# Fused sparse attention and softplus MLP: where in a step the put-off work is taken up

## The chip, the cores and the metric

The kernel runs on one NeuronCore of one Trainium2 chip. The metric is device time in microseconds for one execution of the whole program. The core has five engines that run their own instruction queues side by side: TensorE (matrix products and transposes, PE in the profile; its weight loads are PEld), VectorE (DVE), ScalarE (ACT), GpSimd (POOL) and SyncE (SP, which here issues the DMAs). An instruction waits at the head of its engine's queue until what it reads has been written and what it overwrites has been read.

## The reference

Attention for 8 batches of 8 heads, 576 rows of 64 each, in which each row keeps only the scores that lie within tau of its maximum; the result goes, as 4608 tokens of 512, through two matrices with a softplus between.

```python
scores = scale * np.matmul(q, k.transpose(0, 1, 3, 2))
thresh = np.max(scores, axis=-1, keepdims=True) - tau
scores = np.where(scores >= thresh, scores, -1000000000.0)
attn = np.exp(scores - np.max(scores, axis=-1, keepdims=True))
attn = attn / (np.sum(attn, axis=-1, keepdims=True) + 1e-09)
x = np.matmul(attn, v)          # then (4608, 512)
h = x @ w_in                    # (512, 2048)
g = np.maximum(h, 0.0) + np.log1p(np.exp(-np.abs(h)))
return g @ w_out                # (2048, 512)
```

All of it is float32. The kernel gets that precision from float32r products by splitting an operand into a rounded high part and the rest, a low part, and adding two or three products.

## The kernel before

**Tiles.** A *unit* is one batch and one pair of heads: 32 units. Each has 9 tiles of 128 query rows by 576 keys (4 of each head and one, number 4 of the unit, that holds the last 64 rows of both). The 288 tiles are walked in one loop (L963), one *step* a tile. The feed-forward part is a Python generator (`stream`, L794): it yields after every matmul, so that a step takes a quota of feed-forward matmuls (L967, L985). The quotas follow the table `Q9` over the nine steps of a unit, and 512 tokens make a chunk, which starts a few steps after its attention is done.

**A step.** What a step emits, and in which order, is a string of letters. Steps 0 to 35 use `PAT0`; steps 36 to 287 use `PAT`, which is `ThRlefmpfxSvwp`:

- `T` `weights_T` (L477): TensorE transposes the masked exponentials of this tile (L493; in every second tile of a pair also L490, for the 64 columns left over of both). They land in the PSUM bank that held the tile's scores.
- `h` `weights_hi` (L512): ScalarE casts the transposed weights to their high part gH; in every second tile of a pair it makes one more copy for the left-over columns.
- `R` `row_max` (L446): VectorE takes the maximum of the next tile's scores (negm) and the threshold (thr).
- `l` `weights_lo` (L536): VectorE makes the low part gL of this tile; in second tiles also two short subtractions (out gH).
- `e` `exps` (L453): ScalarE, the exponentials of the next tile. `m` `mask` (L457): VectorE, masks them and sums the row (e_all).
- `f`: half of the quota of feed-forward matmuls (L664, L666, L668 for the first product, L732 for the second).
- `x` `extras` (L908): once in a while the value products of a finished group (`values`, L561, lines L574 to L576), transposes of the next unit's k and q (L375, L377, L383), the reciprocal of the row sums, loads.
- `S` `scores` (L425): TensorE, the scores of the tile after the next (L442), into the bank that this step's h and l have read.
- `v`, `w`: products and weight preparation that occur only early in the kernel.
- `p` `point` (L834): takes up the put-off work that is due.

**Put-off work.** `defer(n, f)` (L828) puts f off by n points. What reads a result of TensorE is put off by one point, so that it isn't queued before the result is near: the casts of the transposed k and q (`qkT`, `queries`, `qkT_rest`: ScalarE, and for q two DMAs by SyncE), the softplus of two finished banks (`softplus`, L679: ScalarE), one point later the split of its result into g high (VectorE) and g low (GpSimd) (`parts_of`, L703), the sums of the second product into acc (`project_out`, L740: VectorE), the output of a value group (`values_out`, L579: ScalarE copies one half of a PSUM bank to xp, VectorE adds the other half), the row sums' way through DRAM (`row_scales_out`, L598: ScalarE, SyncE), and later the scaling and storing of xp (GpSimd, SyncE). None of it issues an instruction of TensorE. The string has two points a step: one behind `m`, one at the end.

**What sets the order.** The framework plans the order of each engine's instructions by emission order and by its own reckoning of when an instruction can start. From step 72 (`TQ`) on, `Queue` (L149) ties each VectorE and each ScalarE instruction behind the one emitted before it, so these two engines keep the order of the string; TensorE's order stays the planner's, which may put a matmul that it reckons ready ahead of one that is emitted earlier and isn't. Value groups are issued by `x` at tiles 2, 5, 7 and, for the last one, at tile 0 of the next unit; transposes of the next unit's k and q at tiles 3, 4, 6 and 8.

ScalarE's exponential and softplus need different activation tables: where one follows the other, a table load stands between.

Of the kernel before, what the change touches and what calls it, by code (L numbers as in the profile page):

```python
# [30 lines left out]
XD = 3  # L31
LS = 4
LAG0 = 5
PAT = "ThRlefmpfxSvwp"
PAT0 = "RMTeShlfpfxvwp"
WD = 4
ST = (1, 3, 4, 4, 5, 6, 6, 8)
# [23 lines left out]
def tile_kernel(ctx: ExitStack, tc: tile.TileContext, q, k, v, tau, w_in, w_out, out):  # L61
# [901 lines left out]
    for g, (cur, t) in enumerate(tiles):  # L963
# [5 lines left out]
        upto = done  # L969
        for step in PAT0 + ("m" if g == TG - 1 else "") if g < TG else PAT:  # L970
            if step == "T":
# [13 lines left out]
            elif step == "f":  # L985
                upto += quota / PAT.count("f")
                while done < upto:
# [51 lines left out]
```

## Time and profile before

| | us |
|---|---|
| median of 3 runs | 1431.99 (1431.76 to 1434.83) |
| profiled execution | 1432.59 |
| its span, first to last instruction | 1430.8 |
| TensorE busy in the span | 1386.3 |
| VectorE busy | 988.3 |
| ScalarE busy | 847.9 |
| GpSimd busy | 588.0 |

In the profile a line of the timeline gives the start in us, the time taken, the engine, the line of the kernel, the operation, what it writes and reads, shapes and the number of instructions merged; in brackets the engine's idle time before it and what ended it. Nearly all VectorE and ScalarE instructions are called through `Queue` and so bear its line, L156: they are told apart by what they write. Matmul ends are modelled, and matmuls overlap: the step from one start to the next tells more than the time taken. Lines of the waits give who waited for whom, the total in us, how often, and the longest.

### The profile page before, as it was taken

Reading aid. Unit: us, or ns where it says so; the run is one execution under the profiler, and the core shown is the slowest. Engines: PE = TensorE matmul, PEld = TensorE weight load, DVE = VectorE, ACT = ScalarE, POOL = GpSimd, SP = SyncE. Lnnn points to the kernel's source line nnn. Section 1 sums busy time; section 2 is a strip of 40 time slices with the busy share of each in tenths; the row PEclk is TensorE's granted clock in tenths of the full one; section 3 lists DMA queues with packets and bytes.
Section 4 is the critical chain, followed back from the end, with each engine's and each line's share of the span. In section 5 each row is a group of like instructions: output and inputs, shape, how many; then the busy total and the mean of one; then the engine's idle time right before and its main releaser. Section 6 shows DMA issues by size and latency. Waiting matters only on the chain.

```text
span 1430.8 us, 23585 instructions
## 1 busy us (share of the span) xinstructions
PE 1386.3 (97%) x7860; PEld 1166.4 (82%) x7860; DVE 988.3 (69%) x2211; ACT 847.9 (59%) x1615; POOL 588.0 (41%) x619
## 2 busy tenths in 40 slices
PE   6988899999999999999999999999999999999998
PEld 4655688788888888888888888888888888788886
DVE  6887688787777777787778777777777777402111
ACT  6766767667666576667665666667666765211110
POOL 3666666534333433344333433344333531323221
PEclk9999999999999999999999999999999999999999
DMA  5766766435333534445443533444434532343421
GB/s 169 222 188 210 221 198 185 126 91 180 111 103 111 155 103 125 120 128 159 117 118 91 165 107 108 127 138 122 122 112 134 157 96 84 101 137 111 135 79 44
DMA packets 131209, 189.94 MB, mean 133 GB/s; under 512 B 35312, under 2 KB 86800, under 8 KB 131088
## 3 DMA queue, kind: packets, MB, share of 16 engines
q1 hardware_dynamic: 131088, 188.43, 45.0%
q8 instruction: 63, 1.03, 0.3%
q14 instruction: 58, 0.48, 0.1%
HBM read 140.51 MB, written 27.41 MB: 117 GB/s over the span
## 4 chain that ended last, share of the span: by engine, by line
PE 82%; DVE 4%; DMA 3%; issue 3%; POOL 3%; ACT 2%; SPq 2%; POOLq 0%; ACTq 0%; DVEq 0%
PE o L732 25%; PE s L442 11%; PE h L666 9%; PE h L668 8%; PE h L664 8%; PE s L493 7%; PE pv L574 4%; PE pv L575 3%; PE tr L383 2%; PE pv L568 2%; DVE e_all L156 1%; DMA qn<-in_q_dram 1%; PE pv L576 1%; PE s L490 1%; DVE negm L156 1%
## 5 line engine op out<-in xcount | busy, mean ns | idle before, releaser
L732 PE MATMUL o<-wo_o,g 128*128 128x512 f32 x1728 | 446.0, 400 | 0.4 <-POOL g L133 0.4
L732 PEld LDWEIGHTS o<-wo_o,g 128*128 128x128 f32 x1728 | 313.5, 188 | 59.7 <-POOL g L133 1.1
L133 POOL TENSOR_TENSOR g<-st,g 128x512 fp32r<-128x512 f32 x144 | 189.7, 1337 | 242.9 <-DVE g L156 224.5
L156 ACT CAST gH<-s 128x512 fp32r<-128x512 f32 (+2 forms) x432 | 179.6, 467 | 144.2 <-PE s L493 118.2
L156 DVE SCALAR_TENSOR_TENSOR e_all<-s,thr,e_all 128x576 f32<-128x576 f32 x288 | 235.2, 817 | 40.7 <-ACT e_all L156 36.4
L666 PE MATMUL h<-xl,wi 128*128 128x512 f32 x576 | 231.9, 403 | 4.6 <-POOL xl L133 4.6
L156 ACT ACTIVATE e_all<-s,negm 128x576 f32<-128x576 f32 x288 | 216.2, 751 | 32.6 <-PE tr L490 15.5
L664 PE MATMUL h<-xh,wi 128*128 128x512 f32 x576 | 232.5, 404 | 2.1 <-ACT xh L156 1.6
L156 DVE TENSOR_REDUCE negm<-s 128x1 f32<-128x576 f32 x288 | 215.6, 748 | 26.1 <-PE s L442 22.5
L668 PE MATMUL h<-xh,wi 128*128 128x512 f32 x576 | 229.0, 398 | 0.0
L156 DVE TENSOR_TENSOR gL<-s,gH 128x512 fp32r<-128x512 f32 (+1 forms) x270 | 169.1, 635 | 47.7 <-ACT gH L156 39.5
L442 PE MATMUL s<-kT,qT 128*128 128x288 f32 x1024 | 194.3, 311 | 7.4 <-ACT gH L156 3.8
L156 DVE CAST g<-st 128x512 fp32r<-128x512 f32 x128 | 57.7, 492 | 170.6 <-ACT st L156 170.6
L442 PEld LDWEIGHTS s<-kT,qT 128*128 128x128 f32 x1024 | 149.7, 191 | 23.6 <-issue 5.3
L493 PE MATMUL s<-identr,e_all 128*128 128x128 f32 x1008 | 151.4, 272 | 0.0
L156 ACT ACT_TABLE_LOAD x111 | 142.4, 1283 | 7.5 <-PE h L668 5.5
L156 ACT ACTIVATE st<-h 128x512 f32<-128x512 f32 x144 | 78.3, 596 | 112.4 <-PE h L668 111.8
L666 PEld LDWEIGHTS h<-xl,wi 128*128 128x128 f32 x576 | 108.4, 188 | 26.8 <-POOL xl L133 6.2
L664 PEld LDWEIGHTS h<-xh,wi 128*128 128x128 f32 x576 | 108.3, 188 | 26.7 <-ACT xh L156 3.4
L493 PEld LDWEIGHTS s<-identr,e_all 128*128 128x128 f32 x1008 | 119.3, 140 | 10.6 <-DVE e_all L156 2.6
L668 PEld LDWEIGHTS h<-xh,wi 128*128 128x128 f32 x576 | 108.3, 188 | 22.3
L574 PE MATMUL pv<-gH,vt 128*128 128x256 f32 (+1 forms) x432 | 118.3, 296 | 0.2 <-ACT gH L156 0.2
(94 smaller groups left out, 1839.4 us busy)
## 6 DMA issues: line engine op xcount, KB each, us to landing
wi<-wi_d SPq DMA_DIRECT2D x144, 512.0 KB
qT<-qT SPq DMA_DIRECT2D x124, 128.0 KB
R<-r_d SPq DMA_DIRECT2D x64, 144.0 KB
kn<-in_k_dram SPq DMA_DIRECT2D x32, 256.0 KB
qn<-in_q_dram SPq DMA_DIRECT2D x32, 256.0 KB
vn<-in_v_dram SPq DMA_DIRECT2D x32, 256.0 KB
wc_i<-in_moe_w_in_dram SPq DMA_DIRECT2D x16, 512.0 KB
wi_d<-wc_i SPq DMA_DIRECT2D x32, 256.0 KB
```

The source lines that it names most:

```text
L133: eng.tensor_tensor(out=out_, in0=in_, in1=hi.bitcast(F32), op=ALU.subtract)
L156: i = getattr(self.eng, name)(*args, **kwargs)
L383: nc.tensor.transpose(pr[:, c * P:(c + 1) * P], src, identr)
L442: i = nc.tensor.matmul(sp[:, hf, 0:HS], lhs, s.kT[j][:, k0 + hf * HS:k0 + (hf + 1) * HS], start=(m == 0), stop=(m == len(parts) - 1))
L493: nc.tensor.matmul(main[:, c, :], e[:, c0:c0 + P], ident, is_transpose=True, start=True, stop=True)
L568: slow.append([lambda c=c: nc.tensor.matmul(o[0:D, 0:n], s.vn[:, 5 * j + c, :], h[:, c, 0:n].bitcast(F32), start=(c == 0), stop=(c == NC)) ...
L574: nc.tensor.matmul(o[:, 0:n], vt[:, c, :], h[:, c, 0:n], start=(c == 0), stop=False)
L575: nc.tensor.matmul(o[:, 0:n], vt[:, c, :], l[:, c, 0:n], start=False, stop=False)
L664: nc.tensor.matmul(h, wi[:, 0, cc, :], u.h[cc], start=(cc == 0), stop=False)
L666: nc.tensor.matmul(h, wi[:, 0, cc, :], u.l[cc], start=False, stop=False)
L668: nc.tensor.matmul(h, wi[:, 1, cc, :], u.h[cc], start=False, stop=(cc == NCC - 1))
L732: nc.tensor.matmul(o, u.g[fc][m // 2][:, sl], wo[fc][:, m % 2, :], start=(n == 0), stop=(n == 3 * QF - 1))
```

## The change

The second point of a step of `PAT` is emitted behind `R` of the next step instead of at the end. The first, behind `m`, stays. A step still has two points, and the work that falls due at each is the same.

```diff
-PAT = "ThRlefmpfxSvwp"
+PAT = "ThRplefmpfxSvw"
 PAT0 = "RMTeShlfpfxvwp"
```

So the order of emission over the border of two steps is, before and after:

```
before  ... m p f x S v w p | T h R l e f m p ...
after   ... m p f x S v w   | T h R p l e f m p ...
```

Nothing else changes. At step 36, the first that uses `PAT`, the point that ends step 35 (`PAT0`) is followed by one behind `R`; the last step has no point behind its products, and what is left is taken up by the points after the loop (L1004).

## The prediction

> **What bounds the kernel now.** I read the page first (the shares of the engines, TensorE far ahead), then the busy time by stage, then who TensorE waits for, and last the timeline of one unit of nine steps. The profiled execution took 1432.59 us: its span of 1430.8 and 1.8 around it. The median of the three timed runs is 1431.99, 0.6 below it; I add my sum to the median.
>
> ```profile
> 295.00:1223.00 928.00, 922.96 (x5536) 808.72 (x5535) 718.08 (x1643) 614.98 (x1143) 355.14 (x370) 1.00 0.42 122
> 129.00:295.00 166.00, 156.32 (x875) 122.35 (x874) 130.45 (x276) 116.33 (x222) 102.28 (x112) 1.00 0.60 180
> ```
>
> ```profile
> PE h L666 <- POOL xl L133: 3.7, 6, 0.6
> ```
>
> The columns after the stage's length are the busy times of PE, PEld, DVE, ACT and POOL. Steps 72 to 287, 24 units of nine, run from about 295 to 1223 us, 38.7 us a unit. There TensorE is busy 922.96 of 928.00 us, and the only wait of it that the profile lists from 295 to 1223 us is 3.7 us in 6 parts, 0.6 the longest. So TensorE is the bound, and at most 5.0 us are to be had there. Steps 36 to 71 use the changed order too and lie in the second stage, with 9.7 us idle. VectorE and ScalarE have room on average; what matters is whether their chain in one step still ends before TensorE gets to the next transposes.
>
> The chain of a step, by the code: transposes T of tile g; ScalarE's casts h read them; VectorE's subtraction l reads the casts; then the mask m of tile g+1, which also needs its exp e; then T of tile g+1. VectorE and ScalarE keep the program's order from step 72 on. One unit's steps, called by their place t in the unit (T at 713.55 is t=7, 716.75 t=8, 720.71 t=0, 725.05 t=1, 729.03 t=2, 733.91 t=3):
>
> ```profile
> 713.08 0.63 PE L732 MATMUL o<-wo_o,g 128*128 128x512 f32 x2
> 713.55 0.60 PE L493 MATMUL s<-identr,e_all 128*128 128x128 f32 x4
> ...
> 716.23 0.69 PE L442 MATMUL s<-kT,qT 128*128 128x288 f32 x4
> 716.75 0.27 PE L490 MATMUL s<-identr,e_all 128*128 128x128 f32 x1
> ...
> 720.71 0.60 PE L493 MATMUL s<-identr,e_all 128*128 128x128 f32 x4
> ...
> 725.05 0.27 PE L490 MATMUL s<-identr,e_all 128*128 128x128 f32 x1
> ...
> 729.03 0.60 PE L493 MATMUL s<-identr,e_all 128*128 128x128 f32 x4
> ...
> 733.91 0.27 PE L490 MATMUL s<-identr,e_all 128*128 128x128 f32 x1
> ```
>
> ```profile
> 715.61 0.82 DVE L156 SCALAR_TENSOR_TENSOR e_all<-s,thr,e_all 128x576 f32<-128x576 f32 x1
> ...
> 716.88 0.49 DVE L156 TENSOR_TENSOR xp<-pv,xp 64x320 f32<-64x320 f32 x1 [0.45 <-ACT xp L156]
> 717.40 0.76 DVE L156 TENSOR_REDUCE negm<-s 128x1 f32<-128x576 f32 x1
> ...
> 718.39 0.69 DVE L156 TENSOR_TENSOR gL<-s,gH 128x512 fp32r<-128x512 f32 x1
> 719.10 0.59 DVE L156 TENSOR_TENSOR gH<-s,gH 64x128 fp32r<-64x128 f32 x2
> 719.72 0.82 DVE L156 SCALAR_TENSOR_TENSOR e_all<-s,thr,e_all 128x576 f32<-128x576 f32 x1
> ...
> 722.90 0.82 DVE L156 SCALAR_TENSOR_TENSOR e_all<-s,thr,e_all 128x576 f32<-128x576 f32 x1
> ...
> 728.01 0.82 DVE L156 SCALAR_TENSOR_TENSOR e_all<-s,thr,e_all 128x576 f32<-128x576 f32 x1
> ...
> 730.92 0.82 DVE L156 SCALAR_TENSOR_TENSOR e_all<-s,thr,e_all 128x576 f32<-128x576 f32 x1
> ```
>
> Masks end at 716.43, 720.54, 723.72, 728.83 and 731.74; the next transposes start at 716.75, 720.71, 725.05, 729.03 and 733.91. The slack is 0.32 (t=7), 0.17 (t=8), 1.33 (t=0), 0.20 (t=1) and 2.17 us (t=2). **The steps with work on the output sums have next to no slack**, though TensorE never visibly waits. The 0.17 is about the shortest gap, so I let T follow m by 0.17.
>
> The two matmuls at 713.08 show a second thing: the feed-forward matmuls of the next step were put ahead of T by the planner that orders TensorE. From 713.08 to 713.55 they took 0.47 us, 0.235 each. The same stands ahead of t=5 (two from 703.70 to 704.16, below). So a T that the planner expects late is covered by work of the next step, as far as it goes.
>
> **The change, part by part.** Nothing is added or removed: every instruction stays, and a step still has two points. The second moves from the end of a step to behind the next step's T, h and R (row maximum). It issues no TensorE instruction, so only its place against h on ScalarE and against R on VectorE changes. T, h and R issue nothing on POOL or SP, so the DMAs and POOL work of the point (swaps of q, row sums, store of x, POOL's subtraction of g) keep their order in those queues; they only start later by what their ScalarE or VectorE input is later.
>
> *Steps 8, 1 and 3 (output sums).* These follow the steps that issue the value products, and they are tiles with two extra subtractions (719.10).
>
> ```profile
> 713.28 0.59 ACT L156 CAST kT<-tr 128x512 fp32r<-128x512 f32 x1 [1.45 <-PE s L442]
> 713.76 0.70 ACT L156 ACTIVATE qT<-tr,qscale 128x512 fp32r<-128x512 f32 x1
> 714.34 0.59 ACT L156 CAST gH<-s 128x512 fp32r<-128x512 f32 x1
> 714.81 0.77 ACT L156 ACTIVATE e_all<-s,negm 128x576 f32<-128x576 f32 x1
> 716.43 0.42 ACT L156 COPY xp<-pv 64x320 f32<-64x320 f32 x1 [0.85 <-PE pv L576]
> 717.50 0.86 ACT L156 CAST gH<-s 128x512 fp32r<-128x512 f32 x2 [0.65 <-PE s L493]
> ```
>
> Now the copy xp (716.43 to 716.85) is free: ScalarE is waiting for T. Behind h, which cannot start before T ends, it runs from about 718.26 (a ScalarE instruction starts some 0.1 before the one ahead ends, as exp at 714.81 before 714.93) to 718.68, and the add xp, which reads it, from 718.70 to 719.19. R does start earlier (at 716.92, when the scores are done, not at 717.40), but VectorE then waits 0.7 us for the copy. l follows at 719.16, not 718.39: **0.77 us later**, and with it the extra subtractions and m, ending at 721.31. T goes to 721.48, 0.77 later than 720.71. With 0.20 slack at t=1 the same growth gives 0.74; t=3 is the same kind, I put it at 0.7.
>
> *Step 7 (casts of k and q).* The two copies start at 713.28 and 713.76 and hold ScalarE until h at 714.34, mostly under the wait for T (ends 714.15). Behind h: h at 714.19, kT 714.67, qT 715.15, exp 715.73 to 716.50, m 716.51 to 717.33 against 716.43. T at 717.50, **0.75 later**. VectorE's R, thr and a sum of the output fit under this.
>
> *Steps 5 and 6.*
>
> ```profile
> 702.96 0.27 ACT L156 CAST kT<-tr 128x128 fp32r<-128x128 f32 x1
> ...
> 703.53 0.70 ACT L156 ACTIVATE qT<-tr,qscale 128x512 fp32r<-128x512 f32 x1
> ...
> 705.28 0.75 ACT L156 ACTIVATE e_all<-s,negm 128x576 f32<-128x576 f32 x1
> 706.05 1.28 ACT L156 ACT_TABLE_LOAD   x1
> 707.34 1.09 ACT L156 ACTIVATE st<-h 128x512 f32<-128x512 f32 x2
> ...
> 708.90 0.86 ACT L156 CAST gH<-s 128x512 fp32r<-128x512 f32 x2
> 709.78 1.28 ACT L156 ACT_TABLE_LOAD   x1
> ```
>
> ```profile
> 703.70 0.39 PE L666 MATMUL h<-xl,wi 128*128 128x512 f32 x1
> ...
> 704.16 0.60 PE L493 MATMUL s<-identr,e_all 128*128 128x128 f32 x4
> ...
> 708.06 0.27 PE L490 MATMUL s<-identr,e_all 128*128 128x128 f32 x1
> ```
>
> ```profile
> 712.36 0.82 DVE L156 SCALAR_TENSOR_TENSOR e_all<-s,thr,e_all 128x576 f32<-128x576 f32 x1
> ```
>
> At t=5 the copies kT to qT take about 1.15 us (702.96 to some 0.1 before qT's end at 704.23). Behind h they push exp by 1.15, m's end to 708.02 (m started 0.03 behind exp: 707.20), T from 708.06 to 708.19: **0.13 later**, since 1.18 was slack. The softplus is then 1.15 later and ends at 709.58; h goes from 708.90 to 709.48, then xp copy (0.42), table load (1.28), exp: the mask ends some 0.4 later than 713.18, at 713.58, T at 713.75, **0.2 later**. In before, the copy lay ahead of h at no cost. (This softplus stands ahead of xp in ScalarE's rows: it is of the first point, which stays where it is. By the quotas in the code 4 of 55 pairs fall to the second; there load, softplus and load, 3.65 us, come between h and exp, at most some 3 us each, 12 in all, which I leave to the upper end.) The casts of g on VectorE (two, behind the softplus) move behind R and still end before l. t=4 has one k cast in a ScalarE that is already back to back: 0.
>
> *Steps 0 and 2* get a k cast (0.27) or a copy of row sums of like size behind h: under their slack, 0.
>
> With TensorE's order as it is, a unit loses 0.77+0.74+0.7+0.75+0.13+0.2 = **3.3 us**, 24 units 79 us: that is the upper end. The lower end: every late T is covered by matmuls pulled forward, and the debt is paid back at t=0 and t=2. Their slack beyond 0.17 and the added 0.27 is 0.89 and 1.73, together 2.6; 0.7 a unit would stay, 16 us, and in units whose softplus falls elsewhere, without the 0.2 and 0.13, less, down to nothing. Between: if only two matmuls (0.47) can be pulled ahead of a T, as both rows show, steps 5, 6, 7 and 8 run uncovered and about 2.4 us a unit are lost. Covering the run up to t=8 wholly asks for 2.6 us, or 11 matmuls, a whole step's worth. I take **1.0 us a unit**, nearer the lower end, because in both quoted places the planner moved what the wait needed. 24 x 1.0 = 24 us. Steps 36 to 71, where the planner is also free to order VectorE and ScalarE, I put at nothing (bounds -4 and +13, four units at 3.3). Sum: 1432 + 24 = **1456 us**.
>
> The Trainium skill (page "TensorE: Matmul & The Clock Gate", section "Why this matters for your kernels") says to keep TensorE's idle gaps under about 3 us, or the clock drops for a window. By that rule stalls of 0.8 us as forecast here cost nothing beyond themselves; the waits of 0.6 us and less in the 24 units, all at clock 1.00, agree but don't test it.
>
> **The rivals.**
>
> ```profile
> 100.00:200.00 100.00, 88.55 (x470) 62.89 (x469) 72.05 (x146) 70.40 (x144) 67.82 (x77) 0.97 0.70 211
> ```
>
> ```profile
> DVE g L156 <- ACT st L156: 57.5, 47, 1.6
> ```
>
> ```profile
> 708.46 1.36 DVE L156 CAST g<-st 128x512 fp32r<-128x512 f32 x2 [1.57 <-ACT st L156]
> ```
>
> 1. *All is covered.* The planner pulls enough matmuls forward, up to 11, and the chain, about as long as TensorE's work, hides. For it: TensorE waited for nothing before although the chain was within 0.2 us in half the steps. Against: the 11. Time: 1432, to 1435.
> 2. *Nothing is covered* (g tiles or PSUM banks not free to run ahead; the bank of a value product is held some 2 us longer, to 719.19 and not 717.37). Time: 1432 + 79 = 1511; with half of it covered 1470.
> 3. *Faster.* VectorE stands 57.5 us in all, 47 times, before the casts of g because softplus is not done, with R queued behind. R in front of them makes R earlier by up to 1.6 us, and exp and T with it. It decides where exp waits for R. In the step of the last row, which waited 1.57 us, the table load before exp ends at 711.06 (709.78 and 1.28), and m starts 1.3 us after that, about the time that exp (0.75) and l's end take, so a much earlier R would gain little there; and TensorE has 5.0 us idle to give back, and perhaps 4 of steps 36 to 71. Time: 1423 to 1429.
> 4. *The clock falls as well.* The granted clock, third from last in the row, was 0.97 where TensorE was busy 88.55 us of 100, and 1.00 in the 24 units; with stalls, 2% of 928 us, most of what that row lost, would add 19 us: 1475.
>
> **How the numbers follow.** Forecast (partly covered, 0.3 to 2 us a unit, 1439 to 1480) 0.57; all covered 0.15; nothing or little covered 0.18; clock 0.04; faster 0.06. A measurement of this kernel tells about 0.2%, 3 us, from no change: faster 0.06, same 0.15, slower 0.79. The range runs from 1432, the foot of the covered case, to 1500, two thirds up the uncovered one (1470 to 1511), so that some 0.06 below and 0.06 above are left out.
>
> **What would show it.** Right: in the timeline the copy xp stands behind the two casts gH, the add xp waits for it, R starts within 0.1 of the scores at t=8, m ends 4.5 us behind T and not 3.8; more feed-forward matmuls between L442 and T; TensorE's waits list DVE e_all in front of L490 and L493, most at t=7 and 8; the stage of the 24 units is longer by about 24 us. Wrong: TensorE's waits unchanged (rival 1), or the chains of t=8 and t=1 not longer (the order isn't kept), or gaps in front of L732 and L664 instead (banks).

## The result

The changed kernel takes 1487.63 us (median of 5 runs, 1485.29 to 1492.84), the kernel before 1434.34 (5 runs, 1431.76 to 1434.88): 1.0386 times as long, 95% interval 1.0372 to 1.0400; the two medians alone give 1.0372. The forecast was 1456 us: the direction was right, and the size less than half of what came, 24 us for some 54.

The loss lies where it was looked for. From the transposes of step 72 to those of step 279, 23 units, the kernel before took 893.5 us (295.49 to 1189.01) and the changed one 944.2 (298.73 to 1242.98): 50.7 us, 2.2 a unit. Steps 36 to 71 took 172.2 for 166.2 us, and what comes before and after differs by under 3 us.

The busy time of the changed kernel over the 24 units, columns as before (length, PE, PEld, DVE, ACT, POOL, clock), and then the first row of the list of whom TensorE waited for:

```profile
298.50:1276.40 977.90, 949.18 (x5531) 799.54 (x5530) 715.30 (x1644) 616.94 (x1143) 353.01 (x370) 1.00 0.40 116
```

```profile
PE o L732 <- ACT qm L156: 17.5, 17, 1.0
```

TensorE's visible idle time grew from 5.0 to 28.7 us. But its busy time grew too, from 922.96 to 949.18, though it runs as many matmuls (5531 records, 5536 before). Matmul ends are modelled and a short wait disappears under the end of the matmul ahead; half of the loss stands in the busy column. The clock stayed at 1.00. A new wait heads the list: feed-forward matmuls L732 that wait for ScalarE's qm. The list of the 24 units has no wait of the transposes for VectorE's masked exponentials (e_all), which the prediction had named as a sign of being right; gaps in front of L732 it had named as one of being wrong.

Step 8 of a unit after the change, in the timelines of TensorE, ScalarE and VectorE (start, time taken):

```profile
745.89 0.27 PE L490 MATMUL s<-identr,e_all 128*128 128x128 f32 x1
...
749.02 0.68 PE L732 MATMUL o<-wo_o,g 128*128 128x512 f32 x2
749.83 0.79 PE L442 MATMUL s<-kT,qT 128*128 128x288 f32 x4
750.46 0.62 PE L732 MATMUL o<-wo_o,g 128*128 128x512 f32 x2
750.92 0.49 PE L493 MATMUL s<-identr,e_all 128*128 128x128 f32 x3
```

```profile
746.63 0.86 ACT L156 CAST gH<-s 128x512 fp32r<-128x512 f32 x2 [1.77 <-DVE negm L156]
747.51 0.42 ACT L156 COPY xp<-pv 64x320 f32<-64x320 f32 x1
```

```profile
745.85 0.76 DVE L156 TENSOR_REDUCE negm<-s 128x1 f32<-128x576 f32 x1
...
747.96 0.49 DVE L156 TENSOR_TENSOR xp<-pv,xp 64x320 f32<-64x320 f32 x1 [1.09 <-ACT xp L156]
748.48 0.69 DVE L156 TENSOR_TENSOR gL<-s,gH 128x512 fp32r<-128x512 f32 x1
749.19 0.59 DVE L156 TENSOR_TENSOR gH<-s,gH 64x128 fp32r<-64x128 f32 x2
749.81 0.82 DVE L156 SCALAR_TENSOR_TENSOR e_all<-s,thr,e_all 128x576 f32<-128x576 f32 x1
```

The copy xp stands behind the casts gH. VectorE has made the maximum early and then waits 1.09 us for the copy; the low part gL starts 2.59 us behind the transposes (748.48 less 745.89), 1.64 before (718.39 less 716.75); the mask ends at 750.63, 4.74 behind the transposes, before 3.79. What the forecast had not: TensorE's scores (749.83) need the bank that the two short subtractions (out gH, until 749.78) read, and stand in front of the matmuls that were pulled forward to cover the wait. The two L732 at 749.02 need 0.47 us, to 749.49; then TensorE stands for 0.34 us although matmuls are ready, and 0.13 of that shows, since the second L732 is modelled to end at 749.70.

The means of all steps 72 to 286, by place in the unit, worked out from the timelines: "step" is from the first transpose (L490 where there is one, else L493) to that of the next step, "chain" from it to the end of the mask. The last column is by how much the prediction's rows put the end of the mask later; it gave no sum, and place 3 is taken like places 1 and 8, "the same kind".

| place | step before | after | chain before | after | change of chain | forecast |
|---|---|---|---|---|---|---|
| 0 | 4.28 | 3.28 | 2.89 | 2.98 | 0.09 | 0.27 |
| 1 | 3.98 | 4.76 | 3.78 | 4.64 | 0.86 | 0.77 |
| 2 | 4.92 | 4.54 | 3.15 | 3.38 | 0.23 | 0.27 |
| 3 | 4.25 | 4.74 | 3.94 | 4.63 | 0.69 | 0.77 |
| 4 | 4.69 | 4.77 | 4.36 | 4.66 | 0.30 | 0 |
| 5 | 3.88 | 4.59 | 2.72 | 3.84 | 1.12 | 1.15 |
| 6 | 5.40 | 4.97 | 4.80 | 4.87 | 0.07 | 0.4 |
| 7 | 3.26 | 4.08 | 2.95 | 3.90 | 0.95 | 0.90 |
| 8 | 4.20 | 5.23 | 3.78 | 4.74 | 0.96 | 0.77 |
| unit | 38.86 | 40.96 | 32.37 | 37.64 | 5.27 | 5.30 |

The chains grew as forecast, within 0.2 us, in all places but two. Places 4 and 6 missed by 0.3 us, one up and one down, so that the sums agree to the hundredth is in part luck. What was wrong is the other part of a step, the time from the mask to the next transposes: 6.5 us a unit before, and 3.3 are left. The forecast needed it to shrink to about 2.2.

Step 5 shows the new wait, TensorE and then ScalarE:

```profile
732.11 0.61 PE L493 MATMUL s<-identr,e_all 128*128 128x128 f32 x4
732.47 0.48 PE L668 MATMUL h<-xh,wi 128*128 128x512 f32 x1
733.98 0.96 PE L732 MATMUL o<-wo_o,g 128*128 128x512 f32 x3 [1.02 <-ACT qm L156]
```

```profile
732.75 0.58 ACT L156 CAST gH<-s 128x512 fp32r<-128x512 f32 x1 [1.61 <-PE s L493]
733.24 0.27 ACT L156 CAST kT<-tr 128x128 fp32r<-128x128 f32 x1
733.39 0.54 ACT L156 ACTIVATE qm<-tr,qscale 128x64 fp32r<-128x64 f32 x2
...
736.45 1.09 ACT L156 ACTIVATE st<-h 128x512 f32<-128x512 f32 x2
```

L668 ends a softplus pair, whose two banks wait for the softplus at 736.45; two more of the four banks of this pool (`GB`, L29) hold the transposed q and the rests of k and q. The sum o needs a bank and gets it when the qm copies, now behind the casts gH, have read the rests. It happens in 17 of the 24 units.

### The profile page after: what moved, and what is told of

Same layout as the page of the kernel before. It is cut to its first block, busy times and chain, and to the rows that moved or that the text cites. A ratio compares the mean times of both kernels' runs of the same rounds, so it can differ in the third digit from the quotient of the medians.

```text
span 1485.2 us, 23531 instructions
## 1 busy us (share of the span) xinstructions
PE 1411.4 (95%) x7860; PEld 1157.2 (78%) x7860; DVE 986.9 (66%) x2211; ACT 849.0 (57%) x1615; POOL 583.6 (39%) x619
## 4 chain that ended last, share of the span: by engine, by line
PE 65%; ACT 10%; DVE 9%; DMA 5%; issue 5%; POOL 3%; SPq 2%; POOLq 0%; ACTq 0%; DVEq 0%
PE o L732 15%; PE s L442 9%; PE h L666 8%; PE h L668 8%; PE h L664 8%; PE s L493 6%; PE pv L574 3%; PE pv L575 3%; ACT gH L156 3%; DVE e_all L156 2%; ACT L156 2%; DVE negm L156 2%; ACT e_all L156 2%; DVE gL L156 1%; PE pv L568 1%
## 5 line engine op out<-in xcount | busy, mean ns | idle before, releaser
L732 PE MATMUL o<-wo_o,g 128*128 128x512 f32 x1728 | 450.7, 402 | 19.0 <-ACT qm L156 17.5
L732 PEld LDWEIGHTS o<-wo_o,g 128*128 128x128 f32 x1728 | 311.1, 189 | 82.6 <-ACT qm L156 22.8
L664 PE MATMUL h<-xh,wi 128*128 128x512 f32 x576 | 234.0, 407 | 3.4 <-ACT xh L156 2.6
L668 PE MATMUL h<-xh,wi 128*128 128x512 f32 x576 | 233.3, 405 | 0.0
L493 PE MATMUL s<-identr,e_all 128*128 128x128 f32 x1008 | 154.7, 276 | 2.0 <-DVE e_all L156 0.2
L493 PEld LDWEIGHTS s<-identr,e_all 128*128 128x128 f32 x1008 | 114.8, 141 | 25.1 <-DVE e_all L156 17.3
L612 POOL TENSOR_TENSOR xp<-xp,R 128x576 f32<-128x576 f32 x32 | 45.9, 1436 | 208.4 <-DMA R<-r_d 171.5
L156 DVE CAST g<-st 128x512 fp32r<-128x512 f32 x128 | 50.5, 437 | 113.1 <-ACT st L156 113.1
L668 PEld LDWEIGHTS h<-xh,wi 128*128 128x128 f32 x576 | 108.8, 189 | 20.3 <-issue 0.4
```

The lines of the kernel that those rows point to most:

```text
L156: i = getattr(self.eng, name)(*args, **kwargs)
L493: nc.tensor.matmul(main[:, c, :], e[:, c0:c0 + P], ident, is_transpose=True, start=True, stop=True)
L612: nc.gpsimd.tensor_tensor(out=s.xp[:, 0:s.n], in0=s.xp[:, 0:s.n], in1=s.R[:, 0:s.n], op=ALU.mult)
L664: nc.tensor.matmul(h, wi[:, 0, cc, :], u.h[cc], start=(cc == 0), stop=False)
L668: nc.tensor.matmul(h, wi[:, 1, cc, :], u.h[cc], start=False, stop=(cc == NCC - 1))
L732: nc.tensor.matmul(o, u.g[fc][m // 2][:, sl], wo[fc][:, m % 2, :], start=(n == 0), stop=(n == 3 * QF - 1))
```

## The experiments

Most kernels put a part of the work back to the end of the step. A tag is given to put-off work, and a new letter `z` takes up, at the end of a step, what is due at the next point and bears a tag of `BACK`. Common to them, against the changed kernel:

```diff
-PAT = "ThRplefmpfxSvw"
+PAT = "ThRplefmpfxSvwz"
...
-    def defer(n, f):
+    def defer(n, f, tag=None):
...
+    def ahead():
+        due = [x for x in later if x[0] <= now["p"] + 1 and x[2] in BACK]
+        later[:] = [x for x in later if not (x[0] <= now["p"] + 1 and x[2] in BACK)]
+        for x in due:
+            x[1]()
...
+            elif step == "z":
+                ahead()
```

The tags: `v` values_out, `k` and `q` the copies of whole k and q, `kr` qkT_rest, `r` row_scales_out, `o` project_out, `g` the casts of g, `s` softplus. Ratios are to the kernel before, with 95% intervals.

**Outputs of the value groups back.** `BACK = ("v",)`.

> As the changed kernel, but the outputs of the value groups (copy xp on ScalarE, add xp on VectorE) are taken up at the end of the step again, in front of T, h and R. Theory (two separate causes: the copy xp behind the casts gH lengthens steps 3, 6, 8 and 1; the copies of k and q behind them lengthen step 7 and hold a PSUM bank in step 5): the chain from T to the end of the mask falls from 4.64 to 3.8 us in steps 1, 3 and 8, the wait of L732 for the copies qm stays; about half of the 53 us goes, 1455 to 1465 us, 1.017 to 1.024 times the kernel before. Rival (one cycle: all the steps together are longer than TensorE's work, and any relief of 2 us a unit frees it): 1433 to 1442 us. Rival (the casts of g and the sums of the output between R and l are to blame): 1480 us or more.

Measured 1463.80 us, 1.0218 (1.0194 to 1.0243). The chains of places 1, 3 and 8 are 3.87, 3.94 and 3.81 us again; L732 still waits for qm, 13.5 us. So 44% of the loss goes, as two causes would have it.

**Copies of k and q back.** `BACK = ("k", "q", "kr")`.

> As the changed kernel, but the copies of the transposed k and q (kT, qT, qm) are taken up at the end of the step again. Theory (two separate causes): the wait of L732 for the copies qm (17.5 us) goes, step 5 falls from 4.6 to 3.9 us and step 7 from 4.1 to about 3.3, steps 1, 3 and 8 stay at 4.7 and more; 1455 to 1465 us, 1.017 to 1.024. Rival (one cycle): 1433 to 1442 us. Rival (casts of g and sums of the output): 1480 us or more.

Measured 1466.49 us, 1.0231 (1.0212 to 1.0249), just above the time expected. The wait for qm is gone, place 5 takes 3.99 us and place 7 3.75, where 3.3 was expected; places 1, 3, 8 stay at 4.74, 4.75 and 5.27. In the list of waits a row shows the scores held by the short subtractions (the lines of this kernel are one further than before, L443 is the scores' line):

```profile
PE s L443 <- DVE gH L157: 4.6, 16, 0.7
```

**Both back.** `BACK = ("v", "k", "q", "kr")`.

> As the changed kernel, but both the outputs of the value groups and the copies of k and q are taken up at the end of the step; behind R stay the casts of g, the sums of the output, the row sums' copy and what comes later. Theory (and the rival of one cycle): 1428 to 1438 us, within 0.4% of the kernel before. Rival (casts of g and sums of the output are to blame): 1465 us or more.

Measured 1435.40 us, 1.0012 (1.0002 to 1.0023): nearly the kernel before. The row maximum ahead of the casts of g and of the sums of the output, which stay behind R, neither gains nor costs anything to speak of. The rival that blamed these falls, and so does the forecast's rival 3: R is earlier behind the transposes in places 2, 4 and 6, by 0.3 to 0.8 us, and the unit is no shorter for it (38.93 us over the 23 units, 38.85 before).

**Only ScalarE's copy xp back.**

```diff
-        defer(1, lambda: values_out(s, g, o))
+        defer(1, lambda: values_copy(s, g, o), "vc")
+        defer(1, lambda: values_add(s, g, o))
...
+BACK = ("vc",)
```

> As the changed kernel, but of a value group's output the copy xp on ScalarE is taken up at the end of the step, and the add xp on VectorE stays behind R. Theory (ScalarE's copy behind the casts is what costs, VectorE's add fits under its wait for the casts): as with the whole output back, 1455 to 1465 us, and the chain of steps 1, 3 and 8 about 3.8 us. Rival (VectorE's 0.49 us in front of l is what costs): the chain falls by 0.3 us at most, 1475 to 1485 us.

Measured 1463.25 us, 1.0212 (1.0190 to 1.0233), as with the whole output back. What costs is the 0.42 us copy on ScalarE behind the casts. With the copy early, the add of 0.49 us on VectorE stands between R and l for nothing, since l waits for the casts anyway; with the copy late, the add is late too, and l stands behind it (747.96, 748.48 in the rows of step 8).

**Only the copies of the rests back.** `BACK = ("kr",)`.

> As the changed kernel, but the copies out of the bank with the transposed rests (one kT, two qm, made in step 5) are taken up at the end of step 4 again; the other copies of k and q and the outputs of the value groups stay behind the casts gH. Theory (step 5's loss is the PSUM bank that the next sum o needs and that the qm copies still read): L732's wait for qm (17.5 us) goes, step 5 falls from 4.6 to about 4.0 us, 1465 to 1473 us. Rival (it is the length of the chain over the copies in step 5 that counts): the qT copy, 0.70 us, stays in the chain, so that at most half of step 5's loss goes, 1478 us or more.

Measured 1468.87 us, 1.0252 (1.0237 to 1.0267): 1.3% of the time, some 19 us, hangs on three short copies, and the wait for qm is gone; place 5 takes 3.91 us.

**All of ScalarE's work back but the softplus.** `BACK = ("vc", "k", "q", "kr", "r")`, with the divided output.

> As the changed kernel, but everything that ScalarE does at the second point except a softplus (copies of k and q, copy xp, the row sums' copy) is taken up at the end of the step, and only VectorE's part (casts of g, sums of the output, add xp) behind R. Theory (only ScalarE's copies cost, VectorE's work fits): 1428 to 1438 us, within 0.4% of the kernel before, since TensorE has at most 5 us idle to give back in the 24 units. Rival (R no longer queued behind VectorE's waits shortens the chain and that is worth something): 1420 to 1427 us.

Measured 1444.32 us, 1.0079 (1.0057 to 1.0100): neither. It is slower than with both back by 0.7%, though VectorE's part had cost nothing in the run with the copy xp back. One place of it can be read in the timeline, VectorE and then GpSimd at the end of a unit:

```profile
453.31 0.69 DVE L157 TENSOR_TENSOR acc<-o,acc 128x512 f32<-128x512 f32 x1
453.91 1.41 DVE L157 TENSOR_SCALAR rs<-sums 128x9 f32<-128x9 f32 x1
455.36 0.22 DVE L157 RECIPROCAL rs<-rs 128x9 f32<-128x9 f32 x1
455.49 0.70 DVE L157 TENSOR_REDUCE negm<-s 128x1 f32<-128x576 f32 x1
```

```profile
453.86 1.43 POOL L134 TENSOR_TENSOR k<-kn,k 128x576 fp32r<-128x576 f32 x1
```

Nine numbers a row take 1.41 us, until GpSimd's subtraction, which started 0.05 earlier, ends (455.29), and the row maximum is late by it. In place 0 there is slack for most of that; place 0 grew by 0.12 us a unit against the run with both back, place 3 by 0.20. Why place 3 grew is open.

**New quotas.** The matmuls of the feed-forward part distributed by the changed kernel's chains.

```diff
-Q9 = (0.9, 1.1, 0.9, 1.1, 1.1, 0.8, 1.2, 0.6, 1.1)
+Q9 = (0.46, 1.43, 0.42, 1.32, 1.28, 0.71, 1.30, 0.69, 1.38)
```

> The changed kernel with the quotas of feed-forward matmuls over the nine steps set anew, by the chains that its trace shows: fewer in steps 0, 2, more in 1, 3, 4 and 8 (Q9 0.46, 1.43, 0.42, 1.32, 1.28, 0.71, 1.30, 0.69, 1.38). Theory (the chains' sum, 37.6 us a unit and 0.1 behind each mask, still fits into TensorE's 38.9; the loss is that each long step lacks matmuls to cover it, and the bank wait of step 5): the bank wait stays, most of the rest goes, 1450 to 1465 us. Rival (the order of work, not the share of matmuls, sets the time; the planner has already moved what can be moved): 1480 to 1495 us.

> The new quotas, and the copies of the rests (kT, qm of step 5) taken up at the end of the step. Theory: both causes are met, 1433 to 1445 us, though the copies xp, and kT and qT of step 7, still stand behind the casts gH. Rival (the share of matmuls does not matter): as with the rests back alone, 1465 us or more.

Measured 1551.49 us, 1.0825 (1.0800 to 1.0850), and with the rests back too 1542.91, 1.0768 (1.0750 to 1.0785): far worse than either theory. The new quotas let softplus pairs fall due at the second point, and ScalarE's timeline shows what that means there:

```profile
706.04 0.85 ACT L156 CAST gH<-s 128x256 fp32r<-128x256 f32 x4 [2.65 <-PE s L496]
706.91 1.28 ACT L156 ACT_TABLE_LOAD   x1
708.20 1.09 ACT L156 ACTIVATE st<-h 128x512 f32<-128x512 f32 x2
709.17 0.59 ACT L156 CAST kT<-tr 128x512 fp32r<-128x512 f32 x1
709.78 1.28 ACT L156 ACT_TABLE_LOAD   x1
711.08 0.74 ACT L156 ACTIVATE e_all<-s,negm 128x576 f32<-128x576 f32 x1
```

Two table loads, the softplus and a copy stand between the casts and the exponential: 711.08 instead of 706.89. Of the 24 such steps among 72 to 286, 22 have chains of 7.3 to 7.5 us. These two runs say nothing of the quotas, but they measure the case that the forecast had priced at some 3 us at most for a pair and put into the upper end: by the quotas 4 of 55 pairs fall there in the changed kernel, and 29 here. The next run takes them away and is 63 us faster than the one with the rests back (1.0768 less 1.0330), 2.2 us a pair.

**New quotas, softplus and the rests back.** `BACK = ("kr", "s")` and the new `Q9`.

> The quotas set anew had moved 29 of the 55 softplus pairs to the second point, where the table load, softplus and the load back stand between h and e (chains of 7.3 to 7.5 us in the trace). Here the new quotas, with a softplus and the copies of the rests taken up at the end of the step. Theory (the share of matmuls in the long steps is what was missing): 1434 to 1450 us. Rival (it is not; the scores behind l and the planner's order hold TensorE whatever the share): 1465 us or more, no better than the rests back alone (1.0252).

Measured 1479.72 us, 1.0330 (1.0314 to 1.0346): worse than the rests back alone. So this distribution of matmuls doesn't give the loss back; places 4, 6 and 7 now take 5.20, 5.40 and 5.14 us with chains of 4.71, 4.61 and 4.96. Whether another would, was not tried.

**Values and rests back, the whole k and q behind.** `BACK = ("v", "kr")`.

> As the changed kernel, but the outputs of the value groups and the copies of the rests (kT, qm of step 5) are taken up at the end of the step; the copies kT and qT of steps 5 and 7 stay behind the casts gH. Theory (of the k and q copies it is the bank of the rests that costs; the others fit under the slack and the pulled matmuls): 1.004 to 1.009, 1438 to 1446 us. Rival (step 7 loses its 0.75 us in each of the 24 units, as the forecast had it): 1.012 or more, 1450 us or more.

Measured 1455.04 us, 1.0168 (1.0142 to 1.0193): the rival in time. Alone, the copies of whole k and q cost 22 us (1.0168 less the 1.0012 of both back, of 1433), 0.9 a unit: places 5 to 7 take 13.62 us, 12.70 with both back, 0.9 more where the forecast had 0.75 for step 7 without any cover. (The profiled execution is the slowest of the four, 1460.92 us, and got to step 72 some 5 us later than that with both back; the places lie behind that.)

**Only the rests behind.** `BACK = ("v", "k", "q", "r", "o", "g")`.

> The reverse: everything at the end of the step as before, and only the copies of the rests (one kT, two qm) behind R and the casts gH in step 5. Theory (the PSUM bank): L732 waits for qm about 0.8 us in the units, 17 in all, whose softplus pair is finished in step 5; 1.010 to 1.016, 1447 to 1456 us. Rival (it costs only together with the other delays): 1.004 or less.

Measured 1444.46 us, 1.0086 (1.0069 to 1.0104), between the two, and without the sign: no L732 waits for qm. The bank wait needs both copies late: it is there in the changed kernel and with the values back, and gone where either the rests or the whole q are early. That the sum o then takes the bank of the whole q is by the code, and no view shows it. Of ScalarE's and VectorE's work all but the rests, and a softplus where one falls due there, stands at the end here as in the kernel before. The chain of place 5 is longer than in that kernel (3.27 us, 2.72 before), and places 5 to 7 take 12.87 us for 12.54, 8 us over 24 units of the 12 lost.

**Values put off one point more.** `BACK = ("k", "q", "kr")` and

```diff
-        defer(1, lambda: values_out(s, g, o))
+        defer(2, lambda: values_out(s, g, o), "v")
```

> The copies of k and q at the end of the step, as in the run that left the outputs of the value groups alone behind R (1.0231), and those outputs put off by one point more, so that the copy xp stands behind the exponential and the add xp behind the mask: later still, but no longer inside the chain T, h, l, m. Theory (the place inside the chain costs, not the lateness): steps 1, 3 and 8 have a chain of 3.8 us again and the time is that of the run with both back, 1.000 to 1.005, 1432 to 1440 us. Rival (lateness costs: the PSUM bank of the value product is held a further 2 us and TensorE runs out of banks): 1.010 or more, 1447 us or more, with waits of TensorE for xp.

Measured 1450.44 us, 1.0123 (1.0104 to 1.0143). The time is the rival's, the mechanism the theory's: the chains of places 1, 3 and 8 are 3.82, 3.94 and 3.80 us, and TensorE doesn't wait for xp, so the place inside the chain was the cause there and the bank isn't. But the work now stands ahead of the next step's R: place 0 has a chain of 4.24 us (2.87 with both back) and place 4 4.85 (4.31). In place 0 it meets GpSimd as above:

```profile
696.91 0.49 DVE L157 TENSOR_TENSOR xp<-pv,xp 64x320 f32<-64x320 f32 x1
697.42 1.27 DVE L157 TENSOR_SCALAR rs<-sums 128x9 f32<-128x9 f32 x1
```

```profile
697.23 1.44 POOL L134 TENSOR_TENSOR k<-kn,k 128x576 fp32r<-128x576 f32 x1
```

No run beats the kernel before; TensorE had 5.0 us idle to give back in the 24 units, and the nearest, both parts back, is 0.12% behind it.

## Why the prediction was wrong

*Right: what bounds the kernel, and which copies lengthen which chains.* TensorE bound it and had nothing to gain. The copy xp behind the casts lengthens steps 1, 3 and 8, the copies of k and q steps 5 and 7; the chain of a unit grew by 5.27 us for 5.30 forecast. Leaving both groups at the end of the step takes the loss away (1.0012), and the copy on ScalarE alone, not the add, makes the first group's part (1.0212 with the copy alone back, 1.0218 with the whole output).

*Wrong: the size of one term, the cover.* The forecast counted 3.3 us a unit of late transposes and held that pulled feed-forward matmuls cover 2.3 of them: "I take 1.0 us a unit, nearer the lower end, because in both quoted places the planner moved what the wait needed." Measured were 2.2 lost, so only 1.1 is covered. The forecast's own case in between, only two matmuls pulled ahead of a T and about 2.4 us a unit lost, was nearer and was passed over for the lower end. In the timelines of steps 72 to 286, 1.0, 1.4, 1.8 and 1.7 feed-forward matmuls on average stand between the scores and the next step's transposes in places 1, 3, 7 and 8 (0.0, 0.5, 0.4 and 0.0 before), and 9.5 over all nine places for 5.0. The 4.6 more, at 0.235 us each, make 1.1 us a unit: an estimate that agrees with the cover measured.

Part by part, from the runs, each against the 1.0012 of both back:

| behind the casts | ratio | us, at 1433 | forecast without cover (24 units) |
|---|---|---|---|
| copy xp (and add xp) | 1.0231 | 31 | 53 (0.77+0.74+0.7) |
| whole k and q | 1.0168 | 22 | 18 (0.75) |
| rests of k and q | 1.0086 | 11 | 8 (0.13+0.2) |
| all three | 1.0386 | 54 | 79 |

The forecast split step 5 between whole q and rests no further; its 0.13 and 0.2 stand in the last row but one. That row's run leaves the casts of g and the sums of the output at the end as well, so the kernel before is its nearer comparison: 12 us. Only for the copies xp was less lost than forecast without cover. Two reasons for that can be read in the runs, and a third is in part argued:

1. *The scores stand in front of the cover.* Before, in the places I quoted, two matmuls stood behind the scores. There the scores were not late. Here the same lateness delays l, and so the scores, which TensorE reaches first (0.34 us in the step shown). I had counted only T as late. An estimate from the two timelines shows how far this goes: take each interval from one matmul's start to the next, less the usual interval behind a matmul of that shape before the change. Of the 50 us that steps 72 to 278 grew by, some 24 then lie in front of the L732 of place 5, some 16 in front of the scores of places 1, 3 and 8, and only 8 in front of the transposes.
2. *A bank.* In step 5 the matmul that should cover needs a bank that the delayed copies hold. The forecast named banks in rival 2, for the value products, and did not count what else of its own step holds one. The changed kernel lists 17.5 us of this wait, and putting the rests back gains 19. But a wait's length is no price: 13.5 us of it vanish between the runs with values back and with values and rests back, and the time falls by 0.5%, 7 us.
3. *Slack that isn't used up.* 1.16 us is left in place 2 and 0.75 in place 5 (steps of 4.54 and 4.59 less their chains 3.38 and 3.84). I let place 2 pay back 1.7. In place 5 the bank wait stands in that time; why place 2 keeps its slack, no run shows.

The costs don't add: the three alone sum to 64 us, together they take 54 beyond both back (1.0386 less 1.0012). Copies of whole k and q beside the copy xp cost 3 us or nothing (1.0252 for 1.0231, intervals that overlap), alone 22.

*The rivals.* All covered, faster: not so. Nothing covered, 1511 us: too much by 23. But the measured time lies beyond the forecast's own case (1439 to 1480) and in the span of this rival with half of it covered or less (1470 to 1511), which had a chance of 0.18; its condition, PSUM banks that aren't free, held for another bank than the one it named. Clock: 1.00 over the 24 units, though their longest listed wait is 1.4 us. The page "TensorE: Matmul & The Clock Gate" of the Trainium skill (section "Why this matters for your kernels") asks for no idle gaps of TensorE above about 3 us, lest the clock drop. The 1.4 us agree with that, and test nothing near 3. Steps 36 to 71, put at nothing with +13 as bound, lost 6 us.

What stays open: how the 1.1 us of cover a unit divides over the late places, what the 0.7% of the run with ScalarE's work back is beyond the 0.12 us in place 0, and whether quotas exist with which the changed order does better.

## What to carry to other kernels

Where a chain over several engines has to end before the bounding engine gets there, look at what stands in the chain, not at how long engines are idle: a 0.42 us copy was free while its engine waited for the chain. Behind the first link it and the add that waits for it made the chains of places 1, 3 and 8 longer by 0.7 to 1.0 us, and cost 31 us for the 96 outputs of the 24 units, 0.3 each. When counting on other work to cover a wait, walk the bounding engine's queue in order: whatever stands ahead of the cover and needs the same late input, and whatever buffer the cover itself needs, takes it away. And read the loss of a pipelined engine from start to start, since short waits hide in its busy time.

## What the runs showed that was not expected

- VectorE's addition of a constant to nine numbers a row (rs) takes 0.16 us at its shortest and up to 1.44 (in the run with the copy xp back) when it starts just behind a GpSimd instruction: 453.91 to 455.32 and 697.42 to 698.69 in the rows above, where GpSimd ends at 455.29 and 698.67. Its mean was 0.35 us over the units before, 0.50 after, 1.01 with the values put off by two points. The Trainium skill (page "SBUF — State Buffer", section "SBUF: two separate sides") has the two engines share a port pair that, for some kinds of VectorE instruction, whoever starts first holds for the whole instruction. In the traces of the kernel before, the changed one and four of the runs, each rs of the units that overlaps a GpSimd instruction ends 0.02 to 0.04 us behind it, which agrees; whether rs is of such a kind, no view here shows.
- The same matmuls showed 26 us more busy time when TensorE had more short waits (949.18 for 922.96 us).
- A softplus pair that falls due half a step later, between the casts and the exponential, makes a step of 4.7 us one of 7.4, by two table loads of 1.28 us each around it.
